# Two transformer-like layers on one core: warm-up matmuls from a constant, a new order of the first loads

## The chip, the cores and the metric

The kernel runs on one core of a Trainium2 chip. The core has five engines, each with its own queue of instructions that it works off in order: TensorE (PE, matmuls), VectorE (DVE), ScalarE (ACT), GpSimd (POOL) and SyncE (SP, which here only issues DMAs). ACT and POOL issue a few DMAs as well. The metric is the time of one execution on the device in microseconds (us); lower is better. The profile gives the span of the instructions within one execution, which is a little shorter than that execution's time.

## What is computed

The input is x, 2048 tokens of 512 values in bf16. A block A (linear attention with 32 heads of 16) and a block B (a two-layer perceptron with 1792 hidden values) are applied twice, with the same weights, each on a layer-normalised input and with a residual sum.

```python
def A(x, wqkv, wo):                       # x: layer-normalised, [2048, 512]
    q, k, v = split(x @ wqkv)             # 32 heads of 16
    phi = lambda t: where(t > 0, t + 1, exp(t)) + 1e-6
    pq, pk = phi(q), phi(k)
    kv, z = sum_s(pk * v), sum_s(pk)      # over all tokens
    return (pq @ kv / (pq @ z + 1e-6)) @ wo
def B(x, w1, b1, w2, b2):
    return gelu(layernorm(x) @ w1 + b1) @ w2 + b2
x = x + A(layernorm(x)); x = x + B(layernorm(x))
x = x + A(layernorm(x)); x = x + B(layernorm(x))
```

## The kernel before

**Tiles.** The tokens lie in 16 tiles of 128, four to a chunk. A chunk of x (512 tokens, 512 KB) is one DMA, `xc0`, `xc1`, `xc2`; the chunk that is worked on first, chunk 3 (`C0=(3, 0, 1, 2)`), is loaded in three pieces: `x0` (tile 12, 128 KB), `x1` (tile 13, 128 KB) and `x2` (tiles 14 and 15, 256 KB). The key weights come in two halves, `wk0` from SP and `wk1` from ACT (256 KB each), the query weights in one piece, `wq` (512 KB). The value weights, `wo`, `w1` and `w2` follow later from POOL. `b1` and `b2` are the two biases; `b2` is spread over all partitions.

**The work on one tile in the first layer.** For tile 12 the operations are named as follows, and the other tiles have the same names with their own number.
- Statistics: `statsA0_12` and `aggrA0_12` on DVE. One tile of the first chunk takes its statistics on ACT instead (`sumA0_..`, `sqA0_..`).
- Normalising: the first four tiles are centred at once (`cenA0_12`), turned, and scaled by the inverse deviation later (`powA0_12` on POOL, then `yscA0_12`). The other tiles are normalised in one step (`normA0_0`).
- Turning to the transposed form: either on PE (`PTA0_12`, four 128-column matmuls against the identity `idp`) with a copy out of PSUM by ACT (`tcA0_12`), or by a DMA transpose that SP issues (`TA0_0`). Tiles 12 to 15 and 1 go by PE, the others of the first layer by DMA.
- Keys: `K0_12`, four matmuls of 512 columns against both halves of the key weights. Then the feature map: an exponential (`expk0_12`) and a relu (`reluk0_12`) on ACT, a minimum (`mink0_12`) and a sum (`phik0_12`) on DVE.
- `G0_12_0`: four matmuls that sum up the outer products of the normalised tile and its keys.
- Queries: `Q0_3_0` to `Q0_3_3` for the tiles of chunk 3, with the same feature map.
- Sums of the keys: `Z0_3` and so on, from a matrix of ones, `onesm`, that DVE writes first (`ones`).

**Dummies.** Before anything else PE runs `warm`: seven matmuls of 512 columns and one of 128 on `onesm`. Their result is not used. POOL prepares the identity (`id0`, `id1`), a constant (`neghalf`) and a block mask (`bdm0`, `bdm1`).

**What sets the order.** The kernel describes all operations with their dependencies, and then plays one written list per engine (`ORDER` in `CONF`). Which engine does an operation is in a second table (`WAY`). A planner walks the lists, with a duration for every operation, only to give out buffers and PSUM banks and to find which semaphore each instruction has to wait for. It does not change the lists. On the chip an engine works off its own list strictly; an instruction that waits holds all that stand behind it. SP's list, for instance, begins

```python
"x0 x1 wk0 x2 wq xc0 xc1 xc2 TA0_0 TA0_3 TA0_2 TA0_8 TA0_4 b2 TA0_6 ..."   # sp
"wk1 sumA0_13 tcA0_12 tcA0_13 sqA0_13 reluk0_12 expk0_12 tcA0_14 ..."      # act
```

The planner's rule for a DMA is that its transfer begins some time after its issue, or when the transfers before it are through, and takes its size over a fixed rate.

The lines of the profile that matter here: L642 and L644 issue the pieces of the first chunk, L638 the chunks, L648 the key weights, L651 the query weights, L1193 `b2`; L680 is the dummies, L783 the turns on PE, L793 the copies behind them, L838 the keys, L856 the queries, L939 the `G` matmuls; L720 the statistics, L760 and L755 the normalising on DVE and on ACT, L770 the DMA transposes; L1119 and L1157 the two matmuls of block B.

Of the kernel before, what the change touches and what calls it, by code (L numbers as in the profile page):

```python
# [6 lines left out]
BF16 = mybir.dt.bfloat16  # L7
# [3 lines left out]
P = 128  # L11
# [99 lines left out]
class Scheduler:  # L111
# [12 lines left out]
    def run(self):  # L124
# [14 lines left out]
        for _ in g.ops:  # L139
# [38 lines left out]
            if e == "sp" or o.sem is not None:  # L178
                if o.name[0] == "T":
                    o.end = max(at + o.lat, bus + 1000.0 if bus > at + 300.0 else 0.0)  # L180
                else:
                    bus = max(at + (1300.0 if at < 1400.0 else 1700.0 if e == "pool" else 900.0), bus) + o.nbytes
                    o.end = bus + o.lat
            else:
                o.end = at + dur + o.lat
# [79 lines left out]
def assign_waits(graph, order, sems, dma_sems):  # L265
# [10 lines left out]
    while len(done) < total:  # L276
        moved = False
        for e in ENGINES:
# [43 lines left out]
    C0=(3, 0, 1, 2), N_WARM=7, ZC=(0, 3), LQ='sp', N_HALF=1, N_K=4, N_Q=3, P_Z0=6.15, N_PB=1, N_PT=8, P_DEN=-50.43,  # L322
# [4 lines left out]
            "warm PTA0_12 PTA0_13 K0_12 K0_13 PTA0_14 Q0_3_0 Q0_3_2 PTA0_15 K0_14 G0_12_0 Q0_3_1 K0_15 G0_13_0 "  # L327
            "G0_14_0 Q0_3_3 PTA0_1 K0_0 K0_1 G0_15_0 K0_3 G0_0_0 K0_2 Q0_0_2 Q0_0_0 G0_1_0 K0_8 Z0_3 K0_4 G0_2_0 "
            "K0_6 G0_3_0 Q0_0_3 K0_7 K0_5 G0_4_0 K0_10 K0_11 Z0_0 K0_9 Q0_1_2 Q0_1_3 Z0_1 Q0_0_1 Q0_1_0 Z0_2 "
            "G0_5_0 G0_6_0 D0_0_3 D0_0_0 G0_7_0 Q0_1_1 D0_0_1 G0_8_0 D0_0_2 G0_9_0 G0_10_0 G0_11_0 G0_11_2 G0_11_1 "  # L330
            "D0_1_0 Q0_2_0 G0_11_3 KV0_0 KV0_1 D0_1_1 ZR0 KV0_2 KV0_3 Q0_2_1 D0_1_2 M0_0 M0_1 M0_2 M0_3 Q0_2_2 "
            "WO0_0_0 WO0_0_1 WO0_0_2 WO0_0_3 D0_1_3 WO0_1_0 WO0_2_0 WO0_3_0 Q0_2_3 WO0_4_0 WO0_7_0 WO0_6_0 PTB0_0 "
            "WO0_5_0 W10_0_5_0 W10_0_1_0 W10_0_9_0 W10_0_6_0 W10_0_2_0 W10_0_3_0 W10_0_12_0 W10_0_7_0 W10_0_0_0 "
            "W10_0_4_0 W10_0_13_0 W10_0_11_0 W10_0_8_0 W10_0_10_0 W20_0_0 W20_1_0 W20_0_7 W20_1_7 W10_0_9_1 "
            "W10_0_1_1 W10_0_7_1 W10_0_8_1 W10_0_5_1 W10_0_6_1 W10_0_12_1 W10_0_0_1 W10_0_13_1 W10_0_3_1 "
            "W10_0_11_1 W10_1_4_0 W10_1_13_0 W10_0_4_1 W10_1_11_0 W10_1_0_0 W10_1_3_0 W10_1_2_0 W10_0_2_1 "
            "W10_1_6_0 WO0_9_0 WO0_8_0 WO0_11_0 W10_1_5_0 W10_1_8_0 W10_1_10_0 WO0_10_0 W10_0_10_1 W10_1_1_0 "
            "W10_1_12_0 W10_1_7_0 W10_1_9_0 W20_7_0 W20_4_0 W20_7_7 W20_4_7 WO0_15_0 W20_5_0 W20_2_0 W20_5_7 "
            "W20_6_0 W10_2_5_0 W10_2_0_0 K1_1 W20_6_7 W20_2_7 K1_0 W10_2_11_0 W10_2_10_0 WO0_12_0 WO0_14_0 "
            "WO0_13_0 W10_2_3_0 W10_2_13_0 W10_2_4_0 W10_2_2_0 W10_2_1_0 W10_2_6_0 W10_2_12_0 W10_2_9_0 W10_2_8_0 "  # L340
            "W10_2_7_0 W20_8_0 W20_9_0 W20_8_7 W20_9_7 W20_3_0 W20_10_0 K1_4 W20_3_7 K1_2 W20_10_7 W10_3_5_0 "
            "W20_11_0 W10_3_7_0 W10_3_1_0 W10_3_8_0 W10_3_3_0 W10_3_10_0 W10_3_0_0 W20_11_7 W10_3_9_0 K1_3 "
            "W10_3_6_0 W10_3_13_0 W10_3_2_0 K1_8 W10_3_11_0 W10_3_12_0 W10_3_4_0 K1_5 G1_0_1 G1_0_3 K1_6 G1_0_0 "
            "W20_12_0 G1_0_2 W20_13_0 W20_12_7 K1_7 W20_13_7 K1_9 K1_10 W20_15_0 W20_14_0 W20_15_7 W20_14_7 G1_1_0 "
            "K1_11 Q1_1_1 Q1_1_0 G1_1_1 G1_1_2 G1_1_3 Q1_0_0 K1_13 K1_12 Q1_1_2 G1_2_1 Q1_0_2 K1_14 K1_15 Q1_0_1 "
            "Q1_1_3 ZH1 Q1_0_3 Z1_3 G1_3_1 G1_2_2 D1_0_0 ZR1 G1_2_0 G1_3_2 D1_0_3 D1_0_1 G1_3_3 G1_3_0 Q1_3_0 "
            "D1_0_2 G1_2_3 KV1_0 KV1_1 KV1_2 Q1_3_1 Q1_3_2 KV1_3 Q1_2_0 M1_3 M1_0 M1_2 M1_1 Q1_2_1 WO1_0_0 Q1_3_3 "
            "WO1_0_1 WO1_1_0 WO1_0_2 WO1_0_3 WO1_2_0 WO1_3_0 Q1_2_2 WO1_5_0 WO1_4_0 PTB1_1 Q1_2_3 PTB1_0 WO1_6_0 "
            "W11_0_13_0 W11_0_5_0 W11_0_12_0 W11_0_4_0 W11_0_11_0 W11_0_6_0 W11_0_3_0 W11_0_0_0 W11_0_10_0 "
            "W11_0_1_0 W11_0_7_0 W11_0_9_0 WO1_7_0 W11_0_8_1 W11_0_4_1 W11_0_10_1 W11_0_8_0 W11_0_1_1 W11_0_5_1 "  # L350
            "W11_0_11_1 W11_0_9_1 W11_0_3_1 W11_0_2_0 W11_0_2_1 W11_0_6_1 W11_0_12_1 W11_0_0_1 W11_0_7_1 "
            "W11_0_13_1 W21_0_0 W21_3_0 W21_3_7 W21_0_7 W21_1_0 WO1_13_0 W21_1_7 W21_2_0 W11_1_8_0 W11_1_5_0 "
            "W11_1_2_0 WO1_14_0 W11_1_0_0 W21_2_7 W11_1_1_0 WO1_12_0 WO1_8_0 W11_1_9_0 W11_1_6_0 WO1_11_0 "
            "W11_1_7_0 WO1_15_0 W11_1_12_0 WO1_10_0 WO1_9_0 W11_1_4_0 W11_1_3_0 W11_1_10_0 W11_1_13_0 W21_7_0 "
            "W11_1_11_0 W21_4_0 W21_7_7 W21_5_0 W21_4_7 W21_5_7 W21_6_0 W11_3_2_0 W11_3_3_0 W11_3_1_0 W11_3_9_0 "
            "W11_3_4_0 W11_3_5_0 W11_3_11_0 W11_3_0_0 W11_3_6_0 W21_6_7 W21_12_0 W11_2_8_0 W11_3_13_0 W11_2_4_0 "
            "W21_14_0 W11_2_5_0 W11_2_7_0 W11_2_11_0 W11_3_7_0 W11_2_1_0 W11_2_6_0 W11_3_10_0 W11_3_8_0 W11_2_10_0 "
            "W11_2_13_0 W11_2_2_0 W11_2_9_0 W11_3_12_0 W11_2_0_0 W11_2_3_0 W21_12_7 W11_2_12_0 W21_8_0 W21_14_7 "
            "W21_8_7 W21_10_0 W21_10_7 W21_9_0 W21_9_7 W21_13_0 W21_13_7 W21_11_0 W21_11_7 W21_15_h0 W21_15_h1",
        "act":  # L360
            "wk1 sumA0_13 tcA0_12 tcA0_13 sqA0_13 reluk0_12 expk0_12 tcA0_14 expk0_13 reluk0_13 expq0_3_0 "
            "reluq0_3_0 tcA0_15 reluk0_14 expk0_14 reluq0_3_2 yscA0_15 reluk0_15 expk0_15 normA0_3 expq0_3_2 "
            "reluq0_3_1 tcA0_1 expq0_3_1 expk0_0 reluk0_1 expk0_1 expq0_3_3 reluq0_3_3 normA0_8 expk0_3 expk0_2 "
            "normA0_6 reluk0_3 expq0_0_2 reluq0_0_2 reluq0_0_0 normA0_7 expk0_8 expk0_4 normA0_5 normA0_10 expk0_6 "
            "reluk0_6 expq0_0_0 expk0_7 expq0_0_3 reluk0_5 expk0_5 expk0_10 expk0_11 reluk0_11 reluk0_9 expk0_9 "
            "reluq0_1_2 expq0_1_2 expq0_1_3 expq0_0_1 reluq0_0_1 expq0_1_0 ln0_0_3 ln0_0_0 rec0_0_3 rec0_0_0 "
            "reluq0_1_1 ln0_0_1 rec0_0_1 expq0_1_1 ln0_0_2 rec0_0_2 ln0_1_0 b1c expq0_2_0 rec0_1_0 ln0_1_1 cpz0 "
            "rec0_1_1 cpm0_0 cpm0_1 cpm0_3 ln0_1_2 rec0_1_2 ln0_1_3 rec0_1_3 expq0_2_1 reluq0_2_1 expq0_2_3 "
            "expq0_2_2 reluq0_2_3 tcB0_0 gelu0_0_5_0 gelu0_0_1_0 gelu0_0_9_0 gelu0_0_6_0 gelu0_0_3_0 gelu0_0_12_0 "
            "gelu0_0_7_0 gelu0_0_2_0 gelu0_0_4_0 gelu0_0_0_0 reluq0_2_2 gelu0_0_11_0 gelu0_0_10_0 gelu0_0_8_0 "  # L370
            "gelu0_0_13_0 gelu0_0_1_1 gelu0_0_7_1 gelu0_0_8_1 gelu0_0_5_1 gelu0_0_9_1 gelu0_0_6_1 gelu0_0_0_1 "
            "gelu0_0_12_1 gelu0_0_11_1 gelu0_0_13_1 gelu0_0_3_1 gelu0_0_4_1 gelu0_1_4_0 gelu0_1_13_0 gelu0_1_0_0 "
            "gelu0_1_11_0 gelu0_0_2_1 gelu0_1_2_0 gelu0_1_3_0 gelu0_1_5_0 gelu0_1_6_0 gelu0_1_10_0 gelu0_1_8_0 "
            "gelu0_1_1_0 gelu0_1_9_0 gelu0_0_10_1 gelu0_1_7_0 gelu0_1_12_0 normB0_11 normA1_1 normB0_9 expk1_1 "
            "expk1_0 gelu0_2_10_0 reluk1_0 gelu0_2_5_0 gelu0_2_0_0 gelu0_2_3_0 gelu0_2_11_0 gelu0_2_13_0 "
            "gelu0_2_2_0 gelu0_2_4_0 gelu0_2_1_0 gelu0_2_6_0 gelu0_2_8_0 gelu0_2_12_0 normB0_13 gelu0_2_7_0 "
            "gelu0_2_9_0 normA1_2 expk1_2 reluk1_2 reluk1_4 gelu0_3_7_0 gelu0_3_1_0 gelu0_3_8_0 normA1_5 normA1_6 "
            "gelu0_3_0_0 gelu0_3_3_0 gelu0_3_5_0 gelu0_3_9_0 gelu0_3_10_0 reluk1_3 normA1_7 gelu0_3_6_0 "
            "gelu0_3_2_0 expk1_3 expk1_8 expk1_4 gelu0_3_13_0 gelu0_3_11_0 gelu0_3_4_0 gelu0_3_12_0 expk1_5 "
            "reluk1_8 expk1_6 reluk1_6 normA1_9 normA1_10 expk1_7 reluk1_7 normA1_11 expk1_9 expk1_10 reluk1_10 "  # L380
            "reluk1_9 normA1_12 expq1_1_1 reluk1_11 expq1_1_0 expk1_11 expk1_13 expk1_12 expq1_1_2 reluk1_13 "
# [138 lines left out]
        "tc_7": "dve", "tc_8": "act", "tc_9": "act", "vepsA0_12": "dve", "vepsA0_13": "pool", "vepsA0_14": "dve",  # L520
        "vepsA0_15": "dve", "vepsA0_9": "pool", "za1_1": "pool", "za1_10": "pool", "za1_11": "pool", "za1_2": "dve",
        "za1_3": "pool", "za1_4": "dve", "za1_5": "pool", "za1_6": "dve", "za1_7": "pool", "za1_8": "pool",
        "za1_9": "pool",
    },
)

# [825 lines left out]
```

## Time and profile before

| what | value |
|---|---|
| runs, us | 331.65, 331.3, 328.13 (median 331.3) |
| profiled execution, us | 330.35 |
| its span, us | 328.6 |
| PE busy | 322.0 us, 98% of the span, 1716 matmuls |
| DVE, ACT, POOL busy | 223.0 (68%), 194.4 (59%), 133.1 (41%) us |
| PE in the chain that ended last | 94% |
| first real matmul (K0_12) | 6.52 us |
| last matmul ends | 326.03 us |

Shares of busy time are means over the whole span. The first tenth is different from the rest: in the first 6.5 us PE runs dummies and two turns, and the other engines wait for data. In a row of the timeline the columns are start, duration, engine, line, operation, what is written and read, how often, and in brackets how long the engine had idled before and what ended that. In a row of waits they are who waited for whom, then us in total, times, and the longest.

### The profile page before, as it was taken

Reading aid. Unit: us, or ns where it says so; the run is one execution under the profiler, and the core shown is the slowest. Engines: PE = TensorE matmul, PEld = TensorE weight load, DVE = VectorE, ACT = ScalarE, POOL = GpSimd, SP = SyncE. Lnnn points to the kernel's source line nnn. Section 1 sums busy time; section 2 is a strip of 40 time slices with the busy share of each in tenths; the row PEclk is TensorE's granted clock in tenths of the full one; section 3 lists DMA queues with packets and bytes.
Section 4 is the critical chain, followed back from the end, with each engine's and each line's share of the span. In section 5 each row is a group of like instructions: output and inputs, shape, how many; then the busy total and the mean of one; then the engine's idle time right before and its main releaser. Section 6 shows DMA issues by size and latency. Waiting matters only on the chain.

```text
span 328.6 us, 4769 instructions
## 1 busy us (share of the span) xinstructions
PE 322.0 (98%) x1716; PEld 159.1 (48%) x1716; DVE 223.0 (68%) x507; ACT 194.4 (59%) x334; POOL 133.1 (41%) x223
## 2 busy tenths in 40 slices
PE   7999999999999999999999999999999999999996
PEld 2444545476544444444444444448644444444444
DVE  4799599999794554575158899999989776100132
ACT  4898769783747055536984377878933452567200
POOL 3366646567447105533047725756903176000000
PEclk9999999999999999999999999999999999999999
DMA  6324593105404300312101110022044214200011
GB/s 231 152 49 98 121 358 149 18 16 97 49 0 66 80 16 3 64 32 48 34 16 32 35 32 0 2 49 50 18 96 99 48 33 97 64 0 2 16 48 64
DMA packets 47027, 20.37 MB, mean 62 GB/s; under 512 B 41948, under 2 KB 45532, under 8 KB 47004
## 3 DMA queue, kind: packets, MB, share of 16 engines
q1 hardware_dynamic: 45676, 15.09, 20.7%
q0 software_dynamic: 1056, 4.72, 4.1%
q8 instruction: 13, 0.21, 0.3%
q10 hardware_dynamic: 272, 0.26, 0.3%
q14 instruction: 10, 0.08, 0.1%
HBM read 8.00 MB, written 2.10 MB: 31 GB/s over the span
## 4 chain that ended last, share of the span: by engine, by line
PE 94%; DMA 2%; DVE 1%; ACT 1%; issue 0%; SPq 0%; ACTq 0%
PE ps L1119 30%; PE ps L1157 29%; PE ps L838 9%; PE ps L1087 8%; PE ps L856 5%; PE ps L971 4%; PE ps L939 3%; PE ps L869 2%; DMA wqkv<-in_A_wqkv_dram 1%; DMA t<-yb 1%; PE ps L1144 1%; PE ps L1063 1%; PE ps L1017 1%; PE ps L994 1%; PE ps L783 0%
## 5 line engine op out<-in xcount | busy, mean ns | idle before, releaser
L1125 ACT ACTIVATE gT<-ps,b1c 128x512 bf16<-128x512 f32 (+1 forms) x140 | 77.0, 601 | 53.8 <-PE ps L1119 53.3
L1119 PE MATMUL ps<-t,w 128*128 128x512 bf16 (+1 forms) x560 | 101.3, 336 | 0.4 <-issue 0.4
L1157 PE MATMUL ps<-w,gT 128*128 128x512 bf16 x434 | 97.3, 379 | 0.0
L1119 PEld LDWEIGHTS ps<-t,w 128*128 128x128 bf16 x560 | 54.6, 98 | 43.6 <-ACT t L793 1.2
L1157 PEld LDWEIGHTS ps<-w,gT 128*128 128x128 bf16 x434 | 42.5, 98 | 50.8
L808 ACT ACTIVATE eb<-ps 128x512 bf16<-128x512 f32 x56 | 32.5, 602 | 31.0 <-PE ps L838 25.6
L735 POOL TENSOR_TENSOR rstd<-veps,neghalf 128x1 f32<-128x1 f32 x64 | 37.8, 598 | 8.3 <-DVE veps L733 5.9
L1167 DVE TENSOR_TENSOR outb<-ps,xsb 128x512 bf16<-128x512 f32 x15 | 10.2, 683 | 40.2 <-PE ps L1157 38.7
L838 PE MATMUL ps<-wqkv,t 128*128 128x512 bf16 x128 | 33.6, 394 | 1.4 <-DMA t<-yb 0.7
L720 DVE BATCH_NORM_STATS2 stats<-xsb 128x6 f32<-128x512 f32 x48 | 32.0, 680 | 0.3
L1087 PE MATMUL ps<-gtb,t 128*128 128x512 bf16 x128 | 30.9, 379 | 0.0
L760 DVE TENSOR_SCALAR yb<-xsb,mv,rstd 128x512 bf16<-128x512 f32 x28 | 16.7, 602 | 13.6 <-POOL rstd L735 13.4
L733 POOL TENSOR_SCALAR veps<-mv 128x1 f32<-128x1 f32 x28 | 7.4, 276 | 43.7 <-DVE mv L722 43.0
L755 ACT ACTIVATE yb<-xsb,nmr,rstd 128x512 bf16<-128x512 f32 x20 | 15.7, 811 | 14.6 <-POOL nmr L752 14.6
L819 ACT ACTIVATE rb<-ps 128x512 bf16<-128x512 f32 x38 | 21.8, 601 | 0.2 <-PE ps L838 0.2
L821 DVE TENSOR_SCALAR eb<-eb 128x512 bf16<-128x512 bf16 x46 | 14.4, 325 | 10.1 <-ACT eb L808 10.0
L725 POOL TENSOR_SCALAR veps<-mv 128x1 f32<-128x1 f32 x32 | 8.8, 274 | 29.1 <-DVE mv L722 27.2
L838 PEld LDWEIGHTS ps<-wqkv,t 128*128 128x128 bf16 x128 | 12.3, 100 | 17.0 <-issue 1.7
L856 PE MATMUL ps<-wqkv,t 128*128 128x512 bf16 x80 | 20.3, 383 | 0.0
L1163 DVE TENSOR_TENSOR xsb<-ps,xsb 128x512 f32<-128x512 f32 x16 | 11.0, 688 | 13.2 <-PE ps L1157 13.1
L1087 PEld LDWEIGHTS ps<-gtb,t 128*128 128x128 bf16 x128 | 12.3, 98 | 15.1 <-DVE mv L722 0.5
L1104 POOL TENSOR_TENSOR xsb<-xsb,b2b 128x512 f32<-128x512 f32 x14 | 17.4, 1255 | 2.8 <-ACT yb L755 1.6
(103 smaller groups left out, 395.2 us busy)
## 6 DMA issues: line engine op xcount, KB each, us to landing
w<-in_B_w_dram POOLq DMA_DIRECT2D x4, 896.0 KB, 9.8
out_dram<-outb SPq DMA_DIRECT2D x15, 128.0 KB, 2.0
t<-in_A_x_dram SPq DMA_DIRECT2D x3, 512.0 KB, 7.3
t<-yb SPq DMA_TRANSPOSE x56, 2.5
wqkv<-in_A_wqkv_dram SPq DMA_DIRECT2D x1, 512.0 KB, 5.8
wo<-in_A_wo_dram POOLq DMA_DIRECT2D x1, 512.0 KB, 4.6
wqkv<-in_A_wqkv_dram POOLq DMA_DIRECT2D x1, 512.0 KB, 7.4
t<-t SPq DMA_TRANSPOSE x20, 2.5
```

The costliest lines, as they stand in the source:

```text
L720: G.op("dve", lambda e: e.bn_stats(stats[:, s.slot, :], src()), 620, reads=src_keys, writes=[k + "s"], tiles=[s, *src_tiles], prio=prio, n ...
L735: G.op("pool", lambda e: e.tensor_tensor(rstd[:, s.slot:s.slot + 1], veps[:, s.slot:s.slot + 1], neghalf[:], op=ALU.pow), 570, reads=[k + ...
L760: G.op("dve", lambda e: e.tensor_scalar(yb[:, y.slot, :], src(), stats[:, s.slot, 2:3] if by_act else mv[:, s.slot, 0:1], rstd[:, s.slot:s ...
L808: G.op("act", lambda e: e.activation(eb[:, et.slot, :], bank(bt), ACT.Exp, scale=factor()), 478, reads=[src_key, *more], writes=[f"e{tag}" ...
L819: G.op("act", lambda e: e.activation(rb[:, rt.slot, :], bank(bt), ACT.Relu, scale=factor()), 478, reads=[src_key, *more], writes=[f"r{tag} ...
L838: ins = e.matmul(bank(b), lhsT=yTa(yT)[:, dt, k * P:(k + 1) * P], rhs=wqkv[:, dt, D:2 * D], start=(dt == 0), stop=(dt == DT - 1))
L856: ins = e.matmul(bank(b), lhsT=yTa(yT)[:, dt, k * P:(k + 1) * P], rhs=wqkv[:, dt, 0:D], start=(dt == 0), stop=(dt == DT - 1))
L1087: ins = e.matmul(bank(wb), lhsT=yTa(pq)[:, kt, k * P:(k + 1) * P], rhs=gtb[:, kt, :], start=(kt == 0), stop=(kt == DT - 1))
L1104: G.op("pool" if on_pool else "dve", lambda e: e.tensor_tensor(xsb[:, st, :], xsb[:, st, :], b2b[:], op=ALU.add), 1120 if on_pool else 600 ...
L1119: ins = e.matmul(bank(b, n), lhsT=w1[:, dt, ft * P:(ft + 1) * P], rhs=yTa(yT)[:, dt, k0 * P:k1 * P], start=(dt == 0), stop=(dt == DT - 1))
L1125: G.op("act", lambda e, ft=ft, b=b, k0=k0, k1=k1, n=n: e.activation(gT[:, g.slot, ft * 512 + k0 * P:ft * 512 + k1 * P], bank(b, n), ACT.Ge ...
L1157: ins = e.matmul(bank(b), lhsT=gT[:, g.slot, ft * 512 + k * P:ft * 512 + (k + 1) * P], rhs=w2[:, ft, :], start=(ft == 0), stop=(ft == FT - 1))
```

## The change

The dummies read a constant 1.0 that the program holds from its start, with a step of zero, instead of `onesm`; there are eight long ones and a short one. Two more groups of short dummies are added: `idle0_0` (six) behind `PTA0_12` and `idle0_1` (two) behind `PTA0_13`. `PTA0_13` has to follow the first of them, and `K0_13` the second.

The planner gets a table `LAND` with a fixed landing time for each of the first nine loads, which it takes whatever the place of the load in the lists. All five lists are written anew, and 14 entries of `WAY` differ; among them the statistics of tile 13 move from ACT to DVE and those of tile 15 from DVE to ACT. The lists of SP and ACT now begin with the orders shown below: `wk1` stands behind `tcA0_12`, `wq` behind `xc2` and `xc0`, `xc1` behind `TA0_0` and `TA0_3`, `b1` ahead of `TA0_0`. `b2` waits for the turns of all tiles and stands behind `Tb1`, the turn of `b1`. On POOL `bdm1` comes before `id1`.

```diff
@@ planner
                 if o.name[0] == "T":
                     o.end = max(at + o.lat, bus + 1000.0 if bus > at + 300.0 else 0.0)
+                elif o.nbytes < 0:
+                    o.end = -o.nbytes
+                    bus = max(bus, o.end - 800.0)
                 else:
@@ CONF
-    C0=(3, 0, 1, 2), N_WARM=7, ...
+    N_WARM2=1, N_IDLE=[6, 2], WK1=1,
+    LAND={'x0': 3210, 'wk1': 5200, 'wk0': 5300, 'x1': 5500, 'wq': 7200, 'x2': 7900, 'xc0': 9700, 'xc1': 11000, 'xc2': 12200},
+    C0=(3, 0, 1, 2), N_WARM=8, ...
@@ ORDER, pe
-            "warm PTA0_12 PTA0_13 K0_12 K0_13 PTA0_14 Q0_3_0 Q0_3_2 PTA0_15 K0_14 G0_12_0 Q0_3_1 K0_15 G0_13_0 "
-            "G0_14_0 Q0_3_3 PTA0_1 K0_0 K0_1 G0_15_0 K0_3 G0_0_0 K0_2 ..."
+            "warm PTA0_12 idle0_0 K0_12 PTA0_13 idle0_1 Q0_3_0 K0_13 Q0_3_1 PTA0_14 G0_12_0 PTA0_15 K0_14 Q0_3_2 "
+            "K0_15 Q0_3_3 G0_13_0 G0_14_0 PTA0_1 K0_0 G0_15_0 K0_1 K0_3 Z0_3 G0_0_0 ..."
@@ ORDER, act
-            "wk1 sumA0_13 tcA0_12 tcA0_13 sqA0_13 reluk0_12 expk0_12 tcA0_14 ... expk0_14 reluq0_3_2 yscA0_15 reluk0_15 expk0_15 normA0_3 ..."
+            "tcA0_12 wk1 expk0_12 tcA0_13 reluk0_12 sumA0_15 expq0_3_0 reluq0_3_0 expk0_13 tcA0_14 reluk0_13 sqA0_15 "
+            "tcA0_15 expk0_14 reluk0_14 reluq0_3_2 expk0_15 reluk0_15 normA0_3 ..."
@@ ORDER, dve
-            "... yscA0_12 statsA0_14 aggrA0_14 cenA0_14 statsA0_15 mink0_12 ... normA0_0 phik0_14 statsA0_6 aggrA0_6 statsA0_2 mink0_15 normA0_1 ..."
+            "... yscA0_12 mink0_12 statsA0_14 yscA0_13 aggrA0_14 ... normA0_0 phik0_14 statsA0_6 statsA0_2 aggrA0_6 mink0_15 normA0_1 ..."
@@ ORDER, pool
-            "bdm0 id0 id1 neghalf powA0_12 ..."
+            "bdm0 neghalf id0 bdm1 id1 powA0_12 ..."
@@ ORDER, sp
-            "x0 x1 wk0 x2 wq xc0 xc1 xc2 TA0_0 TA0_3 TA0_2 TA0_8 TA0_4 b2 TA0_6 TA0_7 TA0_5 TA0_10 TA0_11 TA0_9 b1 Tb1 TB0_1 ..."
+            "x0 x1 x2 wk0 xc2 xc0 wq b1 TA0_0 TA0_3 xc1 TA0_2 TA0_8 TA0_4 TA0_6 TA0_7 TA0_5 TA0_10 TA0_11 TA0_9 Tb1 b2 TB0_1 ..."
@@ the dummies
-        def warm(e):
-            for n in [D] * cf["N_WARM"] + [P]:
-                ins = e.matmul(bank(wu, n), lhsT=onesm[:, 0:P], rhs=onesm[:, 0:n], start=True, stop=True)
+        def run_idle(e, sizes):
+            one = nc.const_aps.tensor(1.0, [P, D], BF16)
+            for n in sizes:
+                ins = e.matmul(bank(wu, n), lhsT=one[:, 0:P], rhs=one[:, 0:n], start=True, stop=True)
             return ins
...
+        idle("warm", [D] * cf["N_WARM"] + [P] * cf["N_WARM2"])
@@ the first layer's tiles
-                    tr = transpose_pe(y, ykey, yT, k, f"yT0_{st}", pr, f"A0_{st}", True)
+                    wait = [held] if held else ()
+                    tr = transpose_pe(y, ykey, yT, k, f"yT0_{st}", pr, f"A0_{st}", True, wait)
+                    held = idle(f"idle{n}_{k}", [P] * cf["N_IDLE"][k], [G.writer[f"yT0_{st}p"]]) if n == 0 and k < 2 else None
...
-                    dma("sp", lambda e: e.dma_start(b2b[:], ...), ["b2b"], prio=-79, name="b2", kb=128, after=[tr])
...
+        dma("sp", lambda e: e.dma_start(b2b[:], ...), ["b2b"], prio=-79, name="b2", kb=128, after=trs)
```

## The prediction

> **What bounds the kernel now.** I read the page first, then what TensorE (PE) waited for, then the first 30 us engine by engine.
>
> ```profile
> PE 322.0 (98%) x1716; PEld 159.1 (48%) x1716; DVE 223.0 (68%) x507; ACT 194.4 (59%) x334; POOL 133.1 (41%) x223
> ```
> ```profile
> PE ps L680 <- DVE onesm L641: 1.5, 1, 1.5
> PE ps L838 <- DMA t<-yb: 0.7, 1, 0.7
> PE ps L1063 <- DVE zb L1000: 0.6, 1, 0.6
> PE ps L838 <- DMA wqkv<-in_A_wqkv_dram: 0.6, 1, 0.6
> ```
> PE is the bound: after its first real matmul it waits some 2 us in all. So the time is the moment at which real work begins, plus any hole made later, plus whatever runs at half rate. The PE timeline of the start:
>
> ```profile
> 6.52 3.57 PE L838 MATMUL ps<-wqkv,t 128*128 128x512 bf16 x8 [0.61 <-DMA wqkv<-in_A_wqkv_dram]
> ...
> 15.14 1.03 PE L838 MATMUL ps<-wqkv,t 128*128 128x512 bf16 x4
> 16.00 1.89 PE L939 MATMUL ps<-pkb,yb 128*128 128x512 bf16 x8
> ...
> 18.59 0.39 PE L783 MATMUL ps<-idp,yb 128*128 128x128 bf16 x4
> ```
> Eight matmuls at 6.52 take 3.57 us, eight equal ones at 16.00 take 1.89: the early ones run at half rate. The step from 0.43 to 0.22 us per matmul lies at 10.9, so 4.4 us of dense work cost 2.2 us extra. The rows are K0_12 (6.52), K0_15 (15.14), G0_13 and G0_14 (16.00) and the turn PTA0_1 (18.59); the last four decide below.
>
> **The change, part by part.**
>
> *Dummies at once.* Eight long and one short at half rate: 8 x 0.43 + 0.11 = 3.5 us from about 0.8 (where ACT and SP begin) instead of 3.1 from 1.51. They end at 4.3; PTA0_12 started at 4.59, when VectorE (DVE) had centred tile 12. Nothing on the path changes. The six idle matmuls behind PTA0_12 (6 x 0.11 = 0.6) lie in a wait; the two behind PTA0_13 (0.2) do not. POOL gets bdm1 (0.86, the row of bdm0) ahead of id1, which then ends at 3.8 instead of 2.9, covered by the same 4.59.
>
> *Key weights, second half (wk1).* The written order of ACT puts it behind tcA0_12, the copy that waits for PTA0_12:
>
> ```profile
> 1.49 0.42 ACTq L648 DMA_DIRECT2D wqkv<-in_A_wqkv_dram  x1
> ...
> 5.25 1.30 ACT L793 ACTIVATE t<-ps 128x512 bf16<-128x512 bf16 x2 [0.57 <-PE ps L783]
> ```
> ```profile
> wo<-in_A_wo_dram POOLq DMA_DIRECT2D x1, 512.0 KB, 4.6
> ...
> t<-in_A_x_dram SPq DMA_DIRECT2D x2, 128.0 KB, 2.5
> wqkv<-in_A_wqkv_dram ACTq DMA_DIRECT2D x1, 256.0 KB, 4.7
> ```
> It was issued at 1.49 and can now go at 5.3 at the earliest. The planner does not see this: LAND gives wk1 a landing of 5.2 whenever it is issued. To landing: at least 2.8 us (2.5 for 128 KB and 0.3 for 128 KB more, at the 1.25 us per 512 KB by which the three chunks landed one after another), at most 4.7, its own row, when it shared the engines as it will again with xc2, xc0 and wq. Bounds 8.1 and 10.0; between, because less is sharing than at 1.49: 9.0. K0_12 waits for it and all of PE stands behind: 9.0 against 6.52, **+2.5** (+1.6 to +3.5).
>
> *Query weights (wq)* now stand behind xc2 and xc0. In the old order 2,048 KB had landed at 9.8; here 2,560 KB stand up to wq, so 11.0. Q0_3_0 asks at 9.0 + 1.7 + 0.4 + 0.2 = 11.3. Nothing, with 0.3 us of cover; up to +1 without it.
>
> *b1* now stands ahead of TA0_0 on SP and waits for b1z, on POOL behind vepsA0_15, which reads sqA0_15. ACT runs that ahead of tcA0_15, which K0_15 needs, so b1z is over before K0_15 (18.3 below), and TA0_3 can't go before 21.3: nothing, 3 us of cover.
>
> *From K0_12 to K0_15.* 8.62 us before. The same seven groups of four lie between, plus one turn and two idle matmuls (0.43 + 0.21 at half rate): 9.3. DVE now measures tile 14 (statsA0_14) behind the first exponential's mink0_12, near 12; its turn PTA0_14 comes at 14.8 on PE, so that is hidden. K0_15 at 18.3, **+0.6**.
>
> *The second chunk (xc1).* SP had sent all of x by 5.0. Now xc1 stands behind TA0_0 and TA0_3, transposes of normalised tiles of chunk 0. A queue does not overtake:
>
> ```profile
> 15.86 10.67 SPq L770 DMA_TRANSPOSE t<-yb  x5
> 26.57 0.58 SPq L1193 DMA_DIRECT2D b2b<-in_B_b_dram  x1
> ```
> b2 had been free to go since tcA0_12 (5.25 + 0.60), but left at 26.57, behind five transposes. DVE meets tile 6, which is of xc1, before it normalises tile 1:
>
> ```profile
> 16.08 0.69 DVE L720 BATCH_NORM_STATS2 stats<-t 128x6 f32<-128x512 bf16 x1
> ...
> 17.71 0.41 DVE L760 TENSOR_SCALAR yb<-t,mv,rstd 128x512 bf16<-128x512 bf16 x1
> ```
> In the new order statsA0_6, statsA0_2, aggrA0_6, mink0_15 and normA0_1 still follow in this sequence; PTA0_1 needs normA0_1, and PE's whole queue needs PTA0_1. The chain, from old durations:
> - K0_15 to TA0_3: 15.14 to 18.17 (exponential, relu, then normA0_3 on ACT, 17.36 + 0.81), 3.0. TA0_3 at 21.3.
> - its issue, 1.2 by SP's transposes (1.19 each): xc1 leaves at 22.5.
> - landing of 512 KB: low 3.0 (2.0 for a 128 KB store, 1.0 for 384 KB more), high 4.6 (wo's row); nearest is the 128 KB load, 2.5 + 0.9 = 3.4: 25.9.
> - statsA0_6 to the end of normA0_1: 16.08 to 18.12, 2.0. PTA0_1 at 28.0 against 18.59, **+9.4**, the +2.5 and +0.6 included.
>
> PE has done the same set of groups up to PTA0_1 in both orders, and was dense behind it; what comes after shifts by the 9.4. DVE (6.5 of 7.6 us busy in 10.9 to 18.5) has no slack to give this back, and POOL's vepsA0_6 stops behind the same tile.
>
> *The clock after the hole.* PE ends G0_14 near 21.7 and idles to 28.0.
>
> ```profile
> 326.10:328.30 2.20, 0.00 (x0) 0.00 (x0) 0.39 (x1) 0.00 (x0) 0.00 (x0) 1.00 0.28 90
> 328.35:328.59 0.24, 0.00 (x0) 0.00 (x0) 0.00 (x0) 0.00 (x0) 0.00 (x0) 0.50 0.00 0
> ```
> The windows at the end show the granted clock (third figure from the right) at 0.50 some 2.3 us after the last matmul; a 6 us hole should do the same. Dense work took 4.4 us to lift it before: **+2.2** (0 if it holds, 3.4 at most if it takes half as long again). The Trainium skill, TensorE: Matmul & The Clock Gate, Why this matters for your kernels, says the same against this order: no gaps over about 3 us between bursts. Part 1 there has the clock return after one to two windows of 3.4 us, an estimate of 1.7 to 3.4 us lost; the sum would be 340.8 to 342.5 by it.
>
> *b2 later.* It stood between transposes, and K0_6's 0.7 us wait for DMA t<-yb is the one behind it: **-0.7** (0 if another transpose is late instead). b2b is first read at 64.5, long after.
>
> The rest of the orders is shuffled without new work; DVE and ACT exchange the statistics of tiles 13 and 15 (0.69 against 0.63 + 0.71). Nothing, ±1.
>
> Sum: 9.4 + 2.2 - 0.7 = +10.9. The profiled execution took 330.35 us (span 328.6 and 1.75 around it): **341.2 us**. The median of the runs shown is 331.3, 0.95 above that execution; runs differ by 3.5 us, so I leave the sum on the profile.
>
> **Rivals.**
> - *The stalls come, the clock is kind.* The gate holds through the hole: 341.2 - 2.2 = 339.0. If the early dummies, turns and idles (0.8 to 5.7 almost without a break) have also lifted it before K0_12 and it lasts the wait of 3.3 us, the 2.2 us at the start goes too: 336.8. Against it is the drop after 2.3 us; for it, that where the step falls may differ by run.
> - *Both loads slow.* wk1 at 10.0 (+1.0), xc1 4.6 (+1.2), no gain from b2 (+0.7): 344.1.
> - *The other side: a load is not held by the waiting instruction ahead of it.* wk1 would go by 1.5, xc1 by 5. K0_12 then starts when tcA0_12 ends, 5.9 (-0.6), PE is busy from 0.8 on and full rate comes by 7.5 (1.6 us of half rate, 0.8 lost instead of 2.2: -1.4), and b2 gives 0.7: 327.7. It decides if wk1 has landed before 5.9 and xc1 before DVE comes to tile 6. The b2 row speaks against it plainly.
> - *The change does what its words say, with small holes only.* Key weights "right behind the first tile" would need SP to send wk0 second; the order has x0, x1, x2, wk0, xc2, xc0, wq. Within 1% needs a hole under 3.3 us, and transfer plus issue of xc1 alone are over 4: 332.
>
> **How the numbers follow.** Forecast 0.58, kind clock 0.25, slow loads 0.12, loads not held 0.03, small holes 0.02. The predicted time is the forecast's. The range takes in the kind clock and the slow loads, with some tenths for the unpriced shuffle: 336.5 to 345.0. A measurement tells about 1%, 3.3 us, from no change. Faster by more needs the loads not held (0.02 of its 0.03); within 1% has the rest of that and the small holes, 0.03; slower 0.95.
>
> **What would show it.** Right: ACT's DMA issue near 5.3; K0_12 near 9.0 with a wait for wqkv over 2 us; on DVE a wait of some 6 us for DMA t<-in_A_x_dram near 20 to 26; PE idle some 6 us before PTA0_1 near 28; slow matmuls again behind it; no 0.7 us wait for DMA t<-yb. Wrong: xc1's issue before 15 us, or PTA0_1 before 22, kills the main term; a granted clock of 1.00 through the hole takes off 2.2; new PE holes after 50 us would mean that the shuffle counts.

## The result, and the profile after

The changed kernel takes 343.9 us (median of 4 runs, 342.76 to 344.09), the kernel before 329.7 (328.13 to 331.65) beside it: a ratio of 1.042, with a 95% interval of 1.034 to 1.050. The profiled execution took 343.88 us, its span is 342.1; before it was 330.35 and 328.6. The runs of the kernel before spread from 327.7 to 331.7 us over all the series, and its profiled execution is one of the longer ones. Between the two profiled executions 13.5 us have to be found, where the prediction had 10.9.

The line of busy time on the page, and what PE waited for in the whole span:

```profile
PE 321.7 (94%) x1694; PEld 159.7 (47%) x1725; DVE 222.1 (65%) x507; ACT 192.6 (56%) x333; POOL 136.4 (40%) x223
```
```profile
PE ps L792 <- DVE yb L769: 6.4, 1, 6.4
PE ps L847 <- DMA wqkv<-in_A_wqkv_dram: 5.7, 1, 5.7
PE ps L1026 <- DVE kvb L1022: 1.6, 1, 1.6
PE ps L1128 <- ACT gT L1134: 0.9, 1, 0.9
```

PE is busy for the same 322 us as before. What is new is two waits of 5.7 and 6.4 us. (The line numbers have moved: L847 was L838, the keys; L792 was L783, the turns on PE; L948 was L939, the `G` matmuls.) The PE timeline of the start shows where they lie:

```profile
0.83 3.27 PE L685 MATMUL ps<-const-bfloat16-1.0 128*128 128x512 bf16 x9 [0.83 <-PEq L1348]
...
11.02 1.89 PE L847 MATMUL ps<-wqkv,t 128*128 128x512 bf16 x4 [5.71 <-DMA wqkv<-in_A_wqkv_dram]
...
19.35 1.04 PE L847 MATMUL ps<-wqkv,t 128*128 128x512 bf16 x4
...
29.70 0.61 PE L792 MATMUL ps<-idp,yb 128*128 128x128 bf16 x4 [6.43 <-DVE yb L769]
30.10 1.91 PE L847 MATMUL ps<-wqkv,t 128*128 128x512 bf16 x4
```

K0_12 stands at 11.02 (6.52 before), K0_15 at 19.35 (15.14), PTA0_1 at 29.70 (18.59). K0_0 behind it takes 1.91 us for four matmuls, K0_15 ahead of the hole took 1.04: half rate again.

The first wait begins on ACT, whose DMA row stands beside the copy tcA0_12; the second on SP and DVE, here with the rows of xc1's issue behind TA0_0 and TA0_3 and of the statistics that wait for it:

```profile
5.00 0.43 ACTq L652 DMA_DIRECT2D wqkv<-in_A_wqkv_dram  x1
```
```profile
20.55 3.55 SPq L779 DMA_TRANSPOSE t<-yb  x2
24.15 0.60 SPq L642 DMA_DIRECT2D t<-in_A_x_dram  x1
```
```profile
27.77 1.29 DVE L729 BATCH_NORM_STATS2 stats<-t 128x6 f32<-128x512 bf16 x2 [6.79 <-DMA t<-in_A_x_dram]
```

The waits of PE name DVE's yb for the second hole; DVE's own row names what DVE waited for, and that is the load. A wait is followed back over the engines until a row is reached that waited for nothing but its place in a queue: here xc1, behind two transposes on SP.

The granted clock by stretches (third figure from the right; ahead of it, after start, end and length, the busy time of PE, its weight loads, DVE, ACT and POOL):

```profile
4.00:6.90 2.90, 0.85 (x12) 0.57 (x10) 1.99 (x8) 0.60 (x1) 1.16 (x2) 1.00 0.92 332
7.00:13.70 6.70, 2.68 (x11) 1.37 (x12) 0.04 (x1) 0.76 (x2) 0.00 (x0) 0.50 0.45 163
13.80:27.40 13.60, 9.17 (x47) 3.99 (x46) 6.30 (x21) 10.86 (x21) 4.43 (x11) 1.00 0.22 58
27.50:34.20 6.70, 4.50 (x14) 1.88 (x15) 5.53 (x17) 2.35 (x4) 2.69 (x8) 0.50 0.12 23
```

The early dummies did lift the clock by 4, and the wait for wk1 threw it away by 7. Ahead of the first change on record the column shows 1.00 whatever the rate (in the kernel before also for 0 to 10.8, where the keys ran at half rate), so there the matmuls' own times decide: the turn PTA0_12 takes 0.40 us at 4.56, the next one, at half rate, 0.63 at 12.70. The hole before PTA0_1 threw the clock away once more, and the 4.5 us from 29.7 to 34.2 ran at half rate.

### The profile page after: what moved, and what is told of

Same layout as the page of the kernel before. It is cut to its first block, busy times and chain, and to the rows that moved or that the text cites. A ratio compares the mean times of both kernels' runs of the same rounds, so it can differ in the third digit from the quotient of the medians.

```text
span 342.1 us, 4753 instructions
## 1 busy us (share of the span) xinstructions
PE 321.7 (94%) x1694; PEld 159.7 (47%) x1725; DVE 222.1 (65%) x507; ACT 192.6 (56%) x333; POOL 136.4 (40%) x223
## 4 chain that ended last, share of the span: by engine, by line
PE 88%; DMA 3%; DVE 3%; ACT 3%; issue 1%; POOL 1%; SPq 0%
PE ps L1128 28%; PE ps L1166 27%; PE ps L1096 8%; PE ps L847 8%; PE ps L980 4%; PE ps L865 4%; PE ps L878 3%; PE ps L948 3%; DMA t<-in_A_x_dram 2%; DMA wqkv<-in_A_wqkv_dram 2%; PE ps L1153 1%; DVE stats L729 1%; ACT eb L817 1%; DVE rd L1054 1%; ACT gT L1134 1%
## 5 line engine op out<-in xcount | busy, mean ns | idle before, releaser
L847 PE MATMUL ps<-wqkv,t 128*128 128x512 bf16 x125 | 33.4, 398 | 5.9 <-DMA wqkv<-in_A_wqkv_dram 5.7
L742 POOL TENSOR_SCALAR veps<-mv 128x1 f32<-128x1 f32 x28 | 7.6, 279 | 61.9 <-DVE mv L731 61.4
L828 ACT ACTIVATE rb<-ps 128x512 bf16<-128x512 f32 x39 | 22.6, 610 | 10.5 <-PE ps L847 10.3
L1172 DVE TENSOR_TENSOR xsb<-ps,xsb 128x512 f32<-128x512 f32 x16 | 10.9, 685 | 21.1 <-PE ps L1166 21.1
L847 PEld LDWEIGHTS ps<-wqkv,t 128*128 128x128 bf16 x128 | 12.6, 101 | 21.7 <-DMA wqkv<-in_A_wqkv_dram 5.9
L948 PE MATMUL ps<-pkb,yb 128*128 128x512 bf16 x62 | 16.7, 395 | 0.1
```

The lines of the kernel that those rows point to most:

```text
L828: G.op("act", lambda e: e.activation(rb[:, rt.slot, :], bank(bt), ACT.Relu, scale=factor()), 478, reads=[src_key, *more], writes=[f"r{tag} ...
L847: ins = e.matmul(bank(b), lhsT=yTa(yT)[:, dt, k * P:(k + 1) * P], rhs=wqkv[:, dt, D:2 * D], start=(dt == 0), stop=(dt == DT - 1))
L948: ins = e.matmul(ps[:, gb.slot + dc, :], lhsT=yb[:, y.slot, dc * P:(dc + 1) * P], rhs=pkb[:, pk.slot, :], start=(st == FIRST), stop=(st == ...
```

## The experiments

The theory for all of them: the loss lies in the places of two loads in the written lists, wk1 on ACT and xc1 on SP, and the clock adds what the second hole costs. The rival: the shuffled lists, the dummies or the clock account for a good part. The first four kernels are edits of the changed one and put loads back.

**wk1 first on ACT again** (`a_wk1`).

```diff
-            "tcA0_12 wk1 expk0_12 tcA0_13 ..."
+            "wk1 tcA0_12 expk0_12 tcA0_13 ..."
```

> The changed kernel with one move: wk1 first on ACT instead of behind tcA0_12. Theory (late loads): wk1 lands by 6.5 us, so K0_12 starts near 6.5 instead of 11.0; but Q0_3_0, second on PE, then waits for wq, which landed at 10.9 in the changed kernel because xc2 and xc0 stand ahead of it. So PE resumes near 11.0 with Q0_3_0 instead of 13.3, and only 2.4 us come back: 341.5 us, with the hole behind xc1 still there. Rival (the wait for wk1 is simply additive): 4.5 us back, 339.4. Rival (the lists' shuffle is the cost, the load is hidden anyway): no change, 343.9.

342.0 us (4 runs, 341.2 to 342.7), ratio 1.0373 (1.0325 to 1.0421). That is 1.9 back.

```profile
7.16 1.02 PE L847 MATMUL ps<-wqkv,t 128*128 128x512 bf16 x4 [1.81 <-DMA wqkv<-in_A_wqkv_dram]
...
11.01 1.45 PE L865 MATMUL ps<-wqkv,t 128*128 128x512 bf16 x4 [2.49 <-DMA wqkv<-in_A_wqkv_dram]
```

K0_12 came 3.9 us earlier, but the first queries behind it then waited 2.5 us for wq, which lands at 11 in either case. wk1's delay had covered wq's. PTA0_1 was 1.1 us earlier (28.61), with the hole of 6.5 us ahead of it as before. The theory's 341.5 lies within the runs, and both rivals (339.4 and 343.9) lie outside.

**xc1 ahead of the transposes** (`a_xc1`).

```diff
-            "x0 x1 x2 wk0 xc2 xc0 wq b1 TA0_0 TA0_3 xc1 TA0_2 ..."
+            "x0 x1 x2 wk0 xc2 xc0 wq xc1 b1 TA0_0 TA0_3 TA0_2 ..."
```

> The changed kernel with one move: xc1 directly behind wq on SP instead of behind TA0_3. Theory: xc1 lands near 12.3, DVE does not wait at statsA0_6, PTA0_1 follows K0_15 (19.4) by some 3.5 us as in the kernel before: 22.8 instead of 29.7, 6.9 us back, and the granted clock does not fall, another 2.3: 334.7 us. Rival (clock falls all the same because of the first hole of 5.7 us): 337. Rival (the hole is covered by slack later): within 1 us of 343.9.

337.1 us (336.3 to 338.2), ratio 1.0227 (1.0179 to 1.0274): 6.8 back, and 2.4 short of the theory.

```profile
12.50 1.89 PE L847 MATMUL ps<-wqkv,t 128*128 128x512 bf16 x4 [6.66 <-DMA wqkv<-in_A_wqkv_dram]
```

The second hole is gone and PTA0_1 runs at full rate at 25.00. But K0_12 came 1.5 us later than in the changed kernel (12.50 against 11.02): wk1, issued from another queue, lands later by about what one more chunk on SP takes (three chunks landed 1.25 us apart in the kernel before). Half rate then lasted 4.3 us behind K0_12 (to 16.8) instead of 2.8. Together these make nearly all of the 2.2 us by which PTA0_1 misses the theory's 22.8. The rival's 337 is met, but the second hole is gone and the clock there is full, so its number is met by chance. `a_act` below asks why wk1 is late.

**Both put back** (`a_both`): the two edits together.

> Both moves together, wq still behind xc2 and xc0. Theory: K0_12 near 6.5, Q0_3_0 near 11.0 behind wq, K0_15 near 17.0, PTA0_1 near 20.5 against 18.6 in the kernel before, no second hole: 331.5 us, 12.4 back, which is more or less the sum of the two single moves. Rival (the shuffle of the lists and the dummies cost something of their own): over 333.5.

334.9 us (332.7 to 335.6), ratio 1.0148 (1.0082 to 1.0213). The theory's 331.5 is missed by more than 3; the rival's bound holds. K0_12 started at 7.59, Q0_3_0 at 11.55 after 1.5 us of waiting for wq, PTA0_1 at 22.10, still 3.5 us behind the kernel before. K0_12 waited for wk0, which stands behind x2 here and landed at 7.5 (2.18 + 5.3), and in these waits the granted clock was at 0.50 again, from 7.5 to 14.3. So there is a further part of the loss, the 5.4 us by which this kernel stays above the kernel before (334.9 against 329.5), in the places of the other loads on SP, wq and wk0 among them, and in the clock that falls in the waits for them. The prediction had costed the place of wq at nothing and had given that of wk0 no term. It can only be seen once wk1 and xc1 are early, and the next kernel shows that it goes with those places.

**All loads as the words of the change have it** (`a_words`): wk0 right behind the first tile, wq behind the second, wk1 first.

```diff
-            "tcA0_12 wk1 expk0_12 tcA0_13 ..."
+            "wk1 tcA0_12 expk0_12 tcA0_13 ..."
-            "x0 x1 x2 wk0 xc2 xc0 wq b1 TA0_0 TA0_3 xc1 TA0_2 ..."
+            "x0 wk0 x1 wq x2 xc0 xc1 xc2 b1 TA0_0 TA0_3 TA0_2 ..."
```

> The loads in the order that the change's words and its table of landings describe: SP x0 wk0 x1 wq x2 xc0 xc1 xc2, wk1 first on ACT; all else as in the changed kernel. Theory: K0_12 near 6.0, wq by 8, so Q0_3_0 does not wait; PE dense from K0_12 on, half rate only until the clock rises, between 7 and 11: 327.5 to 329 us, 0 to 1% under the kernel before. Rival (the rest of the change costs): 331 or more.

329.8 us (10 runs, 328.6 to 331.0), ratio 1.0003 (0.9974 to 1.0033).

```profile
5.85 1.02 PE L847 MATMUL ps<-wqkv,t 128*128 128x512 bf16 x4 [0.46 <-ACT t L802]
...
17.25 0.39 PE L792 MATMUL ps<-idp,yb 128*128 128x128 bf16 x4
```

With nothing but the loads moved, the whole loss is gone, and the rival's 331 lies above the longest run; the theory's 327.5 to 329 is missed by 0.8. What is left of the change (dummies, idles, the shuffled lists, b2 later) is worth nothing that ten runs can tell from zero, though real work begins 0.7 us earlier and PTA0_1 comes 1.3 us earlier than before.

**The other way round: only the loads moved in the kernel before** (`b_late`).

```diff
-            "wk1 sumA0_13 tcA0_12 tcA0_13 ..."
+            "sumA0_13 tcA0_12 wk1 tcA0_13 ..."
-            "x0 x1 wk0 x2 wq xc0 xc1 xc2 TA0_0 TA0_3 TA0_2 ..."
+            "x0 x1 x2 wk0 xc2 xc0 wq TA0_0 TA0_3 xc1 TA0_2 ..."
```

> The kernel before with nothing changed but the places of the loads: SP x0 x1 x2 wk0 xc2 xc0 wq TA0_0 TA0_3 xc1, and wk1 on ACT behind tcA0_12. No new dummies, no other list. Theory (the places of these loads are the whole loss): K0_12 near 11.0, a wait of DVE for xc1 of 6 to 7 us, PTA0_1 near 29 to 30, half rate behind it: 342 to 345 us, as the whole change. Rival (the other lists and the dummies carry a part of it): 340 or less.

344.4 us (342.4 to 345.4), ratio 1.0456 (1.0408 to 1.0504): the changed kernel's time, without any of its other parts.

```profile
11.55 3.59 PE L838 MATMUL ps<-wqkv,t 128*128 128x512 bf16 x8 [5.61 <-DMA wqkv<-in_A_wqkv_dram]
...
30.73 0.61 PE L783 MATMUL ps<-idp,yb 128*128 128x128 bf16 x4 [6.31 <-DVE yb L760]
```

Its PE waits are 5.6 us for the weights (K0_12 at 11.55) and 6.3 us before PTA0_1 (30.73), and the granted clock is 0.50 from 27.5 to 34.2. Together with the kernel above, this shows the cause from both sides: the places of the loads.

**The clock: dummies in the second hole** (`a_fill`). The changed kernel with 24 dummies of 512 columns on PE between G0_14 and PTA0_1.

```diff
-            "... G0_13_0 G0_14_0 PTA0_1 K0_0 ..."
+            "... G0_13_0 G0_14_0 fill PTA0_1 K0_0 ..."
```

> The changed kernel with 24 more dummies of 512 columns (24 x 0.216 = 5.2 us at full rate) on PE between G0_14 and PTA0_1, in the hole behind xc1. Theory (the clock falls because PE idles): the hole is now under 2 us, the granted clock stays at 1.00 through it, the matmuls behind PTA0_1 start 0.216 apart, and the 4.6 us at half rate there give back 2.3: 341.6 us; PTA0_1 itself stays near 29.7. Rival (the clock falls for another reason, or PE is not the bound behind the hole): 343.9. Rival (the dummies push PTA0_1 back): 345 or more.

342.4 us (341.5 to 343.6), ratio 1.0409 (1.0365 to 1.0453): 1.5 us back in the median. Its four runs overlap those of the changed kernel (342.8 to 344.1), so the times alone don't settle it.

```profile
31.59 0.38 PE L800 MATMUL ps<-idp,yb 128*128 128x128 bf16 x4 [1.90 <-DVE yb L777]
31.81 1.03 PE L855 MATMUL ps<-wqkv,t 128*128 128x512 bf16 x4
```

With the hole filled, K0_0 takes 1.03 us instead of 1.91: the half rate behind PTA0_1 is the idle PE's doing, and dummies prevent it. In this execution the clock came up later at the start (at 16.7 instead of 13.8), so K0_15 was 1.4 us later and PTA0_1 1.9; so the 2.3 us of the clock's term are borne out in their mechanism, and by the times only as 1.5.

**Why wk1 took 6.0 us** (`a_act`). In the changed kernel the DMA queue of ACT (q10) carries wk1 alone. From 5 to 8 us, the three microseconds behind its issue, and from 8 to 11, the queues that moved anything were:

```profile
q1 hardware_dynamic: 389, 1.09, 95.7%
...
wqkv<-in_A_wqkv_dram ACTq DMA_DIRECT2D x1, 256.0 KB, 6.0
```
```profile
q1 hardware_dynamic: 467, 0.47, 44.5%
q10 hardware_dynamic: 272, 0.26, 24.8%
```

The columns are packets, MB and the share of 16 engines. For 3 us SP's queue q1 has the engines to itself, and q10 does not move a packet. Its first one starts at 8.27. From 8 on q1 has 0.47 MB left, less than wq alone, and the two queues share the engines. So wk1 came behind all that SP had issued ahead except the last load, wq, and ran beside that one. The edit: ACT issues xc2, xc0 and wq as well, behind wk1, so that SP's queue runs out early.

```diff
-            "tcA0_12 wk1 expk0_12 tcA0_13 ..."
+            "tcA0_12 wk1 xc2 xc0 wq expk0_12 tcA0_13 ..."
-            "x0 x1 x2 wk0 xc2 xc0 wq b1 TA0_0 TA0_3 xc1 ..."
+            "x0 x1 x2 wk0 b1 TA0_0 TA0_3 xc1 ..."
```

> The changed kernel, but ACT issues xc2, xc0 and wq too, right behind wk1, instead of SP ahead of it: when wk1 is issued, SP's queue q1 holds only what is left of x0, x1, x2 and wk0. What is disputed is why wk1 took 6.0 us to land. Theory: its queue q10 moves next to nothing until q1 has run out. q1 then runs out near 6, q10 starts within 1.3 us of the issue at 5.0, wk1 lands 2.8 to 3.2 us after it, and K0_12 starts at 7.8 to 8.3. Rival: a load that ACT issues beside its activation is slow by itself, whatever stands on SP: q10 again moves nothing for some 3 us, the landing takes 4.5 to 6.0, K0_12 starts at 9.5 to 11. In both wq lands last, near 11.7 to 13, Q0_3_0 waits for it, and the hole before PTA0_1 stays at 6 to 7 us, so that the time says little (340.5 to 344).

One execution. From the DMA issues of the first 9 us and the PE timeline:

```profile
wqkv<-in_A_wqkv_dram ACTq DMA_DIRECT2D x1, 256.0 KB, 2.8
```
```profile
7.88 1.89 PE L847 MATMUL ps<-wqkv,t 128*128 128x512 bf16 x4 [2.56 <-DMA wqkv<-in_A_wqkv_dram]
```

Issued at 5.02, first packet of q10 at 6.10, landed in 2.8 us, K0_12 at 7.88: on wk1 the theory in each number, the rival in none. The time, 345.4, lies above what both had given (340.5 to 344): wq landed at 13.2, and in this execution the granted clock was 0.50 from 7.5 to 17.7.

The Trainium skill, DMA: Bandwidth & Descriptors, Queues, rings and completion order, says that each DMA engine goes round the queue rows that have work, packet by packet. By that wk1 would have shared the engines from its issue on. The trace differs at first, with 1.09 MB of q1 and nothing of q10 in 3 us, and agrees from 8.27 on, when both move. Whether the packets of wk1 stood ready in their queue by then, the trace doesn't show; which step holds them back (making the descriptors, or serving them) stays open.

**The dummies alone in the kernel before** (`b_dum`). Eight long ones and one short on the constant, from 0.83; the lists stay.

```diff
-    N_WARM=7, ...
+    N_WARM=8, ...
-                ins = e.matmul(bank(wu, n), lhsT=onesm[:, 0:P], rhs=onesm[:, 0:n], start=True, stop=True)
+                ins = e.matmul(bank(wu, n), lhsT=one[:, 0:P], rhs=one[:, 0:n], start=True, stop=True)
```

> The kernel before with the dummies alone: eight long ones and a short one from the constant, from 0.83 us, no idle groups, all lists as before. Theory: the clock rises by 4 or 5 us where it did not before, but between the dummies' end (4.4) and K0_12 (6.5) PE has only two turns, so in a part of the runs it falls again: between 0 and 2.2 us better, 328.5 us in the median. Rival (half rate until dense real work has run for a window, whatever the dummies): 329.5, no change.

330.0 us (12 runs, 329.3 to 333.6), ratio 1.0047 (1.0019 to 1.0074): no gain, rather a loss of half a per cent. The theory's 328.5 is missed; the rival's 329.5 is nearer, but not for its reason, as the rows of the start show. It is better by all that early dummies could give:

```profile
5.78 1.90 PE L839 MATMUL ps<-wqkv,t 128*128 128x512 bf16 x8
...
16.22 0.39 PE L784 MATMUL ps<-idp,yb 128*128 128x128 bf16 x4
```

The first keys run at full rate, and PTA0_1 is 2.4 us earlier than in the profiled execution of the kernel before. Against that execution nearly all of the gain is given back at one place, the first block B (here L1120):

```profile
75.09 4.97 PE L1120 MATMUL ps<-t,w 128*128 128x256 bf16 x44
81.99 2.21 PE L1120 MATMUL ps<-t,w 128*128 128x512 bf16 x11 [1.93 <-ACT gT L1126]
```

The kernel before ran this stretch without a break from 77.76 on; of the 2.4 us, 0.6 was left at the last matmul's end (325.46 against 326.03). ACT, which the row names, had ended its gelus at 81.31 (80.10 + 1.21). What came last was a DMA transpose: issued at 76.7, landed after 5.2 us, which gives 81.9. These are the queues and issues from 76.2 to 79.2 in b_dum, and from 78.6 to 81.1 in the kernel before, the same point of the work:

```profile
q8 instruction: 1, 0.02, 2.6%
...
t<-yb SPq DMA_TRANSPOSE x2, 3.8
```
```profile
t<-yb SPq DMA_TRANSPOSE x2, 2.5
```

In b_dum a packet of the instruction queue q8 lies in the stretch, at 78.67, and the median of the two transposes is 3.8 us instead of 2.5: the first still landed in 2.5, the one beside the packet in 5.2. In the kernel before no such packet lies there; it comes at 81.26, and makes the next two transposes late (4.6 and 3.8 us), for which PE does not wait.

That packet and late transpose belong together shows in all twelve profiled executions. Of 63 transposes of tiles with a packet of q8 starting within the 2.2 us behind their issue, 53 took over 3 us to land, with a median of 3.9; of the 849 others 31 did, with a median of 2.5. What remains open is why the median of the runs is no better than that of the kernel before: the profiled execution of `b_dum` is 0.6 us shorter than the other kernel's, the median of its runs 0.7 longer.

**The same with eight short dummies behind PTA0_13** (`b_idle`).

```diff
-            "warm PTA0_12 PTA0_13 K0_12 ..."
+            "warm PTA0_12 PTA0_13 idle K0_12 ..."
```

> The same as the dummies alone, with one more group of eight short dummies behind PTA0_13, which fill PE until the key weights land (6.5). Theory: PE is busy from 0.83 on with no hole over 0.4 us, so the clock is up at K0_12 and stays up in all runs: 2 us better than the slow executions of the kernel before, 328.0 us and a narrower spread. Rival (the added dummies delay K0_12 by their own 0.4 to 0.8 us and take the gain): 329.

329.5 us (12 runs, 329.3 to 332.1), ratio 1.0029 (1.0004 to 1.0054). PTA0_1 at 16.70, and a break of 1.4 us at 81.77: the same picture. The theory's 328.0 is missed and the rival is near: K0_12 starts at 6.60, 0.8 us later than in `b_dum`, behind the added dummies. Keeping PE busy between the turns adds nothing.

**Moving the instruction packet** (`c_128`). The eight dummies of `b_dum` cut into 32 of 128 columns: as long, but more instructions.

```diff
-            for n in [D] * cf["N_WARM"] + [P]:
+            for n in [P] * (4 * cf["N_WARM"]) + [P]:
```

> The kernel before with early dummies from the constant (as in the second-last experiment), but the eight of 512 columns cut into 32 of 128: the same columns, 24 matmuls and 24 weight loads more. Theory: the early clock's 2.2 us were given back because a 16 KB packet of the instruction queue q8 (it moves 16 KB about every 256 instructions of PE) met the last DMA transposes of the second layer's first chunk, whose landing went from 2.5 to 5.2 us and held PE for 1.9 us at 81.99. 48 more PE instructions bring that packet some 3.5 to 4 us earlier against the work (to about 75, PE runs some 12 instructions in a us there), ahead of those two transposes: the matmuls behind the wait at about 80 instead of 81.99, no wait over 1 us there, the last matmul 1.5 to 2 us earlier, a median of 328.0 (327.3 to 328.6). Rival 1: the wait is one of the order of the work (a gelu, the issue pace of the transposes), and stays at 1.9 whatever the instructions: 329.5 to 330.3. Rival 2: the packet moves but meets other transposes or another later wait takes the gain back: the wait near 80 is gone, the time still 329 to 330.

330.7 us (12 runs, 329.4 to 333.1), ratio 1.0045 (1.0012 to 1.0078). Rival 2 is the nearest: the packet now lies at 75.7, between 75 and 77.9, where `b_dum` has none, and the transposes issued there take 3.6 us to land. The wait near 80 shrank from 1.9 to 1.0 us and did not go, as rival 2 had said that it would, and two further waits of 0.6 us came in at L1120, at 227 and 246. That the packet moves with the number of PE instructions, and that transposes beside it land late, is what the two kernels show together; that nothing else eats the 2.4 us is not shown.

## Why the prediction was right, and where its sizes were off

The forecast was the mechanism that ran: two loads held by instructions ahead of them in their engines' lists, PE behind both, and half rate behind the second hole. Its time, 341.2, is 2.7 below the median and its range (336.5 to 345.0) holds it.

| step | forecast | measured |
|---|---|---|
| wk1 issued, us | 5.3 | 5.00 |
| wk1's landing, us | 2.8 to 4.7, taken 3.7 | 6.0 |
| K0_12 | 9.0 (+2.5) | 11.02 (+4.5) |
| K0_12 to K0_15, us | 9.3 | 8.33 |
| K0_15 to TA0_3, us | 3.0 | 3.5 |
| xc1's landing, us | 3.4 | 3.6 |
| landing to PTA0_1, us | 2.0 | 1.95 |
| PTA0_1 | 28.0 (+9.4) | 29.70 (+11.1) |
| half rate behind the hole, us | 2.2 | 2.3 |
| wait behind b2, us | -0.7 | -0.7 |

- *The mis-sized term is wk1's landing.* The working put it "between, because less is sharing than at 1.49", and 11.02 for K0_12 lies above even its upper bound of 10.0. The sum looked at how many bytes share the engines, where the question was which queue is served first: all that SP had issued ahead except wq came before it, 3.3 us without one packet of its own. wk1 landed at 11.0 (5.00 + 6.0), with wq, the last of SP's (3.64 + 7.2 = 10.8). The prediction had that moment one paragraph on, 11.0 for wq, and did not use it for wk1.
- *Rival "slow loads"* had wk1 at 10.0 and xc1 at 4.6: right for wk1 in its sign, wrong for xc1, which took 3.6, near the 3.4 of the nearest row.
- *From K0_12 to K0_15* the path was 1.0 us shorter than forecast: the clock rose 2.8 us behind K0_12 (13.8), where 4.4 had been taken from the run before. That hid half of the error on wk1, and it was luck: with the same lists up to there, `a_fill` had the rise 5.5 us behind K0_12.
- *wq's "0.3 us of cover"* held, but only because K0_12 was late: `a_wk1` and `a_both` show 2.5 and 1.5 us of waiting for wq as soon as wk1 is early. A cover that consists of another wait costs when that wait is taken away, and the prediction did not price that.
- *The clock.* The rival with the kind clock is out: 0.50 from 27.5 to 34.2. Its second half, dummies that lift the clock before K0_12, came true and was worth nothing, since the wait for wk1 outlasted it. From PTA0_1 to the last matmul's end it is 309.9 us (29.70 to 339.58) against 307.4 before (18.59 to 326.03), +2.4. Half rate makes 2.3 of it (29.7 to 34.2); PE's other waits there went from 1.7 to 2.5 us, with new ones at kvb (1.6) and in block B (0.9) in place of the one behind b2. That leaves 0.7 us of gain that stays unexplained.
- *The shuffle, "nothing, ±1"*, holds: `a_words` and `b_late` bound it from both sides. The prediction's sign against it, new holes of PE behind 50 us, did come: all seven kernels with the changed lists wait 0.6 to 1.6 us for kvb, and none of the five with the old lists does. But these five wait 0.4 to 0.6 us for zb, which the seven don't, and `a_words` shows that the exchange is not worth a loss that ten runs can tell.

## What to carry to other kernels

In a written list a load is as early as the instruction ahead of it lets it be, and a load on a second queue may stand behind nearly all that the first queue has in flight: before moving a load later, look up what both queues hold at that moment, not how much bandwidth is free. Follow a hole of the busiest engine back over the rows of the engines that it names until one waits for nothing but its place. And before spending work on an earlier start, make sure that the next fixed wait does not swallow it: in the profiled executions 2.4 us won at 16 us had shrunk to 0.6 behind 82.

## What the runs showed of the hardware that was not expected

- *A second queue got nothing for 3 us.* wk1's 256 KB took 6.0 us behind SP's backlog in the changed kernel (first packet 3.3 us behind the issue, landed at 11), 2.8 us without the backlog (`a_act`, first packet after 1.1 us), and with one chunk more on SP K0_12 came 1.5 us later still (`a_xc1`).
- *The clock's windows are short, and their place differs by run.* In the changed kernel 3.3 us of dummies from 0.83 sufficed to lift it, and by 7.0, 1.7 us behind PE's last dummy (5.31), it was gone. The same dummies did not lift it in `a_fill` and `a_xc1`, where the first rise came at 16.7 and 16.8. Full rate came 2.8 us behind K0_12 in the changed kernel, some 10 us behind it in `a_act`, where PE idled 2.8 us in between.
- *The clock changes on a grid.* The changes on record in the changed kernel lie at 3.55, 6.96, 13.79, 27.44 and 34.27, which are 1, 2, 4 and 2 steps of 3.41 us apart. The other ten executions that record changes have whole numbers of the same step between them, on a grid that starts elsewhere in each. Up to 37 us, a step at half rate that PE filled to 81% or more, by its busy time in the trace, ended in full rate in every execution, one of 76% or less in none, and of three at 79 or 80% one did. A step at full rate that PE filled to 38% or less ended in half rate, one of 47% or more in none.
- *Instruction packets cost transposes.* The page of the profile counts 13 packets of 16 KB on q8 before and 14 with 48 PE instructions more (`c_128`); a DMA transpose beside one landed in 5.2 us where 2.5 is usual (`b_dum`). The Trainium skill, Runtime: NRT & Kernel Launch, Instruction fetch mechanics, has blocks of 16 KB, 256 instructions each, and calls their cost mostly hidden. The trace agrees on the size and, by the 3,432 matmuls and weight loads of the kernel before in 13 packets, roughly on the count (264 each); the cost was not hidden from the transposes.
